# Four heads' 64x64 products at a time, three stores behind the branch, and another order of attention

## The chip, the cores and the metric

The kernel runs on one core of a Trainium2 chip. The metric is the time of one launch in microseconds (us), as the device reports it; the kernel before took 660.73 us (median of three runs, 658.44 to 661.97).

## What is computed

A linear attention with a decaying state, then two feed-forward layers; the second mixes four domains by given shares.

```python
for t in range(S):                     # B, H, S, D = 2, 8, 768, 48
    cur = einsum('bhd,bhe->bhde', u[None] * kt, vt)
    y[:, :, t] = einsum('bhd,bhde->bhe', rt, state + cur)
    state = wt[:, :, :, None] * state + einsum('bhd,bhe->bhde', kt, vt)
x = y as (1536, 384)
h = x @ w_in                           # 384 x 2048
x = where(h > 0, h, exp(min(h, 0)) - 1) @ w_out
p = domain_probs / (domain_probs.sum(-1, keepdims=True) + 1e-09)
for e in range(4):                     # w1 384 x 1024, w2 1024 x 384
    out += p[:, e:e + 1] * (maximum(x @ w1[e], 0) @ w2[e])
```

## The kernel before

**Attention** goes by 12 chunks of 128 time steps, six of each batch, taken in turn from the two batches. Eight heads lie as four pairs: a pair's two heads (48 rows each) stand on partitions 0 to 63 and 64 to 127. One chunk is a handful of pieces, each with a two-letter name in the table `ORDER`: loads of the decays (`iw`), of k and r (`ik`) and of v (`lv`); two scans on DVE (`su` L293, `pr` L301); k and r times the scans (`kd`, `rd`) and k times r (`g`); the transposed k (`tr` L316); the scores (`pa` L324), masked by `am`; the scores of a step with itself (`ow` L331: one 128x128 product for each pair, whose weights `ublock` hold u in two diagonal blocks of 64); these times v (`vo`, tile `bv`); the state's update (`pp` L358, added by `us` L365); the values (`py`: a state part L374, 64x64, then a part from the masked scores L378, 128x64, summed in one bank of PSUM); the sum with `bv` (`ys` L382); and the split of the result in two words for exact products (`xs`), spread over idle partitions by two transfers (`xd` L260).

**The first feed-forward layer** is 48 steps (four quarters of the hidden width, three blocks of four chunks, four columns each): `h` (L408, nine products of 128x512), `e` and `el` (exp, the greater of the two, the split), `z` (L429, nine products), and `dr`, which empties three banks after four steps. Its weights come in 32 pieces: `wl` loads, `wa`, `wb`, `wc` split each 64-bit word into two numbers (DVE L226, L227, ACT, POOL).

`ORDER` names every piece of the first part in the order in which each engine gets its instructions; a letter behind a number names the engine (A ACT, D DVE, P POOL, M and S mixtures for the two masks). Each engine takes its instructions strictly in that order. PSUM has eight banks: one holds limits for the scans, seven are handed out in the order in which they came free, so that a product waits for the reader of the bank that it is given. At the start `kept_busy` has PE do 11 products of 128x256 that nobody reads (L162).

**The second layer** (`experts`) is one long row of products with numbers as due times: `product` (L597, three products into a chain's bank `chain_a` to `chain_e`), `taken` (DVE or ACT reads that bank into `terms`, L609, L612, L614), `hidden_hi` (ACT) and `hidden_lo` (DVE L651), which split a hidden block into `hl`, `second` (L658, three products each), `weighted` (L667) and `added` (L673, L675). A chain's bank is written on by the next product of the chain once `taken` has read it. `load_blocks`, `split_hi` and `split_lo` prepare the weights, those of the first two blocks already beside the first layer. Nine stores (h = 7) go out from `added`, on SP's queue (L677).

At the end every engine loads a flag and branches: where decays lie out of a safe range, everything is computed again in a slower way (`recur`). With the inputs here this branch is not taken.

Of the kernel before, what the change touches and what calls it, by code (L numbers as in the profile page):

```python
# [11 lines left out]
F32 = mybir.dt.float32  # L12
# [74 lines left out]
ys9 e5 pa10 rd11P ow10 ws10A e6 dr15D pa11 el6D am10M am11S el5P py10 xs9P h7 z4 xd9 vo10 h17 g11D e7 el7P ys10 z5
xs10P ow11 vo11 h16 z6 e16 py11 e17 ys11 z7 xs11D el16P z16 xd8 xd10 dr7A h19 el17D h18 e18 xd11 | el18P e19 el19D
z17 h8 h9 e9 el9P z18 e8 el8P h11 h10 wl8 z19 e11 z8 e10 el11D wa8D el10D h21 wl11 z9 wa11D dr19D wl10 wb8P wl9 wa10D
h20 wb10D wb11P wc10D e20 z10 e21 el20D h22 wa9D z11 dr11A e22 wb9D wc8D wc11P z20 wl24 wl26 wl27 wc9D wa24D el21P  # L90
h23 el22D wa26D wb24D h24 e23 wb26D el23P z21 wa27D e24 wl25 el24P h25 z22 wa25D e25 wc26P wc24P h26 z23 el25D wl12
wl15 wb25P z24 wc25D e26 dr23D wb27D h27 wl14 wa15D el26D z25 e27 wa14D h28 wb15P e28 el27P h29 z26 wa12D wc27P el28D
h30 wb12P z27 wl28 e29 wc15D dr27D e30 wb14P wl13 wc14D el29P z28 h31 wl31 e31 el30D h32 el31D z29 e32 h35 wa13D z30
el32P wa28D wc12D wl30 wb13P e35 h33 el35D wb28P wa31D wc13P z32 e33 wl29 el33D z31 h34 wb31D dr31D wa30D wc28P wa29D
e34 h36 el34D z33 e36 el36P wb29D h37 wb30P z34 h38 wc30D e37 el37P z35 dr35D wc29P e38 z36 h39 wc31P el38P z37 h40
e40 e39 el39D el40D h41 z38 h42 e41 el41D h43 z39 e42 el42P dr39D z40 e43 h44 z41 e44 el43D h45 el44D z42 h46 e45 z43
el45P e46 el46P h47 dr43D z44 e47 z45 el47D z46 z47 dr47D
""".split()


@with_exitstack
def kernel_body(ctx, tc, wkr, vv, uu, w_in, w_out, w1, w2, dp, out):
# [145 lines left out]
    def heads_bank():  # L248
        return heads(bank())
# [674 lines left out]
```

## Time and profile before

| | us |
|---|---|
| three runs, median (lowest, highest) | 660.73 (658.44, 661.97) |
| the profiled execution, its own time | 660.07 |
| its span, first to last instruction | 658.3 |
| PE busy in the span | 638.9 |
| DVE busy | 490.6 |
| POOL busy | 362.4 |
| ACT busy | 302.2 |

The span is the time between the first and the last instruction; 1.8 us of the execution's own time lie outside it. Busy shares are means over stages with different limits: in the first 90 us DVE and PE take turns in holding the work up, later PE alone is full.

### The profile page before, as it was taken

The numbers are of one execution on the slowest core, as the hardware profiler recorded it, in microseconds if no ns is written. First come the engines' busy times: TensorE is split into PE (matmuls) and PEld (weight loads), VectorE is DVE, ScalarE is ACT, GpSimd is POOL, SyncE is SP. The second block draws the span as 40 slices with busy tenths as digits, with TensorE's granted clock in tenths as the row PEclk, the third lists the DMA queues.
The fourth block names the chain that finished last, engine by engine and source line by source line (L and its number), as shares of the span: only waits on it lengthen the run. The fifth ranks groups of instructions, "written<-read, shape, count | busy, mean of one in ns | idle before, by whom it ended". The sixth has DMA issues, their size and how long they took to land.

```text
span 658.3 us, 9122 instructions
## 1 busy us (share of the span) xinstructions
PE 638.9 (97%) x3330; PEld 524.0 (80%) x3330; DVE 490.6 (75%) x703; ACT 302.2 (46%) x582; POOL 362.4 (55%) x322
## 2 busy tenths in 40 slices
PE   7989999999999999999999999999999999999994
PEld 6878778888888778888888878878788788787883
DVE  7799999335766834599786877977967868768782
ACT  2436666455856557448343523423532434343230
POOL 5775555412242353546552765876876867744352
PEclk8789999999999999999999999999999999999998
DMA  8768550040322400001212112003130121300012
GB/s 312 220 199 289 164 174 0 17 154 1 96 73 72 144 3 1 1 0 49 88 42 72 53 53 88 25 16 105 42 104 17 41 72 34 120 0 1 0 49 102
DMA packets 20970, 50.92 MB, mean 77 GB/s; under 512 B 2680, under 2 KB 3880, under 8 KB 20916
## 3 DMA queue, kind: packets, MB, share of 16 engines
q1 hardware_dynamic: 20772, 50.25, 23.9%
q8 instruction: 28, 0.46, 0.3%
q14 instruction: 26, 0.21, 0.1%
q10 hardware_dynamic: 144, 0.00, 0.0%
HBM read 46.68 MB, written 2.38 MB: 75 GB/s over the span
## 4 chain that ended last, share of the span: by engine, by line
PE 71%; DVE 16%; issue 3%; ACT 3%; DMA 0%; SPq 0%; DVEq 0%; ACTq 0%
PE second L658 24%; PE bank L429 11%; PE bank L408 10%; PE chain_a L597 8%; PE chain_b L597 5%; PE chain_p L629 4%; PE chain_c L597 3%; PE chain_d L597 2%; DVE scaled L667 2%; PE chain_e L597 1%; DVE raw L227 1%; DVE terms L609 1%; DVE hl L651 1%; DVE e L416 1%; DVE t L226 1%
## 5 line engine op out<-in xcount | busy, mean ns | idle before, releaser
L658 PE MATMUL second<-hl,w2s 128*128 128x512 f32 x864 | 230.9, 389 | 0.1
L658 PEld LDWEIGHTS second<-hl,w2s 128*128 128x128 f32 x864 | 162.0, 188 | 34.4 <-DVE hl L190 0.5
L675 POOL TENSOR_TENSOR x<-scaled,x 128x512 f32<-128x512 f32 x60 | 86.9, 1470 | 93.2 <-DVE scaled L667 93.2
L408 PE MATMUL bank<-x,w 128*128 128x512 f32 x432 | 105.2, 392 | 1.3 <-DVE e L416 0.9
L429 PE MATMUL bank<-hl,w 128*128 128x512 f32 x432 | 105.0, 391 | 0.6 <-ACT hl L194 0.4
L651 DVE SCALAR_TENSOR_TENSOR hl<-terms,hl 128x512 fp32r<-128x512 f32 x92 | 91.5, 997 | 11.0 <-ACT hl L645 11.0
L408 PEld LDWEIGHTS bank<-x,w 128*128 128x128 f32 x432 | 80.4, 188 | 19.1 <-DVE e L416 1.5
L429 PEld LDWEIGHTS bank<-hl,w 128*128 128x128 f32 x432 | 80.6, 188 | 18.5 <-ACT hl L194 0.8
L190 POOL TENSOR_TENSOR sums<-blocks,sums 128x512 fp32r<-128x512 f32 (+1 forms) x56 | 75.3, 1356 | 26.9 <-ACT sums L194 26.9
L515 POOL TENSOR_TENSOR blocks<-blocks 128x256 f32<-128x256 f32 x84 | 71.8, 875 | 1.2 <-DMA blocks<-in_w 0.5
L190 POOL TENSOR_TENSOR hl<-e,hl 128x512 fp32r<-128x512 f32 x21 | 27.5, 1314 | 73.9 <-ACT hl L194 73.9
L612 ACT ACTIVATE terms<-chain_b 128x512 f32<-128x512 f32 x28 | 16.8, 600 | 106.1 <-PE chain_b L597 106.1
L645 ACT ACTIVATE hl<-terms 128x512 fp32r<-128x512 f32 x96 | 58.1, 623 | 14.1 <-PE second L658 6.8
L416 DVE SCALAR_TENSOR_TENSOR e<-e,bank 128x512 f32<-128x512 f32 x48 | 32.3, 681 | 39.0 <-ACT e L412 39.0
L612 ACT ACTIVATE terms<-chain_a 128x512 f32<-128x512 f32 x28 | 16.8, 598 | 80.6 <-PE chain_a L597 80.6
L597 PE MATMUL chain_a<-x,sums 128*128 128x512 f32 x168 | 47.3, 390 | 0.2 <-DVE terms L609 0.2
L411 ACT ACTIVATE e<-bank 128x512 f32<-128x512 f32 x48 | 28.4, 592 | 32.8 <-PE bank L408 29.8
L609 DVE TENSOR_TENSOR terms<-terms,chain_a 128x512 f32<-128x512 f32 x42 | 28.8, 685 | 19.1 <-PE chain_a L597 19.0
L667 DVE TENSOR_TENSOR scaled<-second,pr 128x512 f32<-128x512 f32 x60 | 40.5, 686 | 3.0 <-PE second L658 1.8
L194 ACT ACTIVATE hl<-e 128x512 fp32r<-128x512 f32 x48 | 30.0, 629 | 24.7 <-DVE e L416 21.8
L232 POOL TENSOR_TENSOR raw<-raw,t 128x384 int32<-128x384 int32 x20 | 21.7, 1099 | 33.2 <-ACT t L228 33.2
L597 PEld LDWEIGHTS chain_a<-x,sums 128*128 128x128 f32 x168 | 31.5, 188 | 7.1 <-DVE terms L609 0.6
(117 smaller groups left out, 996.8 us busy)
## 6 DMA issues: line engine op xcount, KB each, us to landing
kr<-in_wkr SPq DMA_DIRECT2D x12, 512.0 KB, 4.8
raw<-in_w_in SPq DMA_DIRECT2D x16, 384.0 KB, 3.8
raw<-in_w_out SPq DMA_DIRECT2D x16, 384.0 KB, 3.6
blocks<-in_w SPq DMA_DIRECT2D x16, 384.0 KB, 3.5
raw<-in_w SPq DMA_DIRECT2D x16, 384.0 KB, 4.2
v<-in_vv SPq DMA_DIRECT2D x12, 456.0 KB, 5.7
w<-in_wkr SPq DMA_DIRECT2D x12, 262.5 KB, 4.5
gw<-in_wkr SPq DMA_DIRECT2D x12, 262.0 KB, 2.8
```

The costliest lines, as they stand in the source:

```text
L190: engines[e].tensor_tensor(o, a, b.bitcast(F32), ALU.subtract)
L408: nc.tensor.matmul(ph, lhsT=wi[:, sa, f, kk, :], rhs=x[:, kk, c0:c0 + nch, sm], start=(kk == 0 and i == 0), stop=(kk == 2 and i == 2))
L416: nc.vector.scalar_tensor_tensor(b["e"], b["e"], -1.0, b["ph"], ALU.add, ALU.max)
L429: nc.tensor.matmul(pxs[q, bl][d][:, :cols], lhsT=wo[:, sa, f, d * P:(d + 1) * P], rhs=b["t"][:, sm], start=(f == 0 and i == 0), stop=(f == ...
L515: nc.gpsimd.tensor_tensor(*(places(blocks[u], p) for p in (r, a, c)), ALU.subtract if op == "-" else ALU.add)
L597: nc.tensor.matmul(banks[c], lhsT=weights(u, r, sa), rhs=tokens(r)[:, sm], start=r in HEADS and i == 0, stop=i == 2, skip_group_check=True)
L609: nc.vector.tensor_tensor(out, a, b, o)
L645: nc.scalar.activation(out=hls[f, b][:, 0], in_=results[f, b], func=AF.Copy if weighted else AF.Relu)
L651: nc.vector.scalar_tensor_tensor(hls[f, b][:, 1], results[f, b], 0.0, hls[f, b][:, 0].bitcast(F32), ALU.max, ALU.subtract)
L658: nc.tensor.matmul(sums[d], lhsT=w[:, sa, f, d * P:(d + 1) * P], rhs=hls[4 * h + f, b][:, sm], start=f == i == 0, stop=f == 3 and i == 2)
L667: nc.vector.tensor_tensor(o, sums[d], prs[h // 2, b], ALU.mult)
L675: nc.gpsimd.tensor_tensor(x2[:, d, s], scaled[d], x2[:, d, s], ALU.add)
```

## The change

Own scores: `ublock` is now 64 columns wide, and each head's product is 48x64 on its own quarter of the array. `QUARTERS` takes two pairs at a time, and turns the second pair round: its upper head's result goes to the lower partitions, and the other way. So four heads in a row use four different quarters of the array, two of them into one bank and two into another. The state part of the values is done in the same way; the part from the masked scores has the same products as before in another order, into the two banks. `vo` and `ys` thereby become two instructions of 128x256 each. v comes turned round from the host for the odd pairs, and rows of `w_in` are permuted to suit.

`kept_busy` is gone: a token `n2` now puts two unread products of 128x256 into the next bank that is handed out, ahead of that bank's own products. There are 14 of them in the new `ORDER`. In the second layer `hidden_lo`, where it falls due next to product 10, now comes 2.6 places later instead of 0.6; the first two blocks of its weights are split 20 places later. The last three stores stand behind the branch.

```diff
 ORDER = """
-iw0 ik0 su0 wl4 iw1 kd0D ik1 iw7 pr0 lv0 g0P su1 wa4D tr0A rd0P kd1P iw2 ow0 wb4P ik2 pa0 lv1 pr1 vo0 su2 pp0 rd1P
+wl4 wa4D iw1 iw0 su1 ik1 wl0 pr1 ik0 wb4P ik3 kd1P su0 rd1P n2 pa1 tr1A wa0D iw3 pr0 wl2 g1D lv1 rd0D iw5 n2 ow1 kd0P
...
+        for _ in range(extra.pop() if extra else 0):
+            nc.tensor.matmul(t[:, 0:IDLE], lhsT=idle[:, 0:P], rhs=idle[:, 0:IDLE], start=True, stop=True)
...
-    for p in range(NPAIR):
-        nc.scalar.activation(out=ublock[:, p], in_=half, func=AF.Copy, scale=u_sb[:, p])
+    ublock = apool.tile([P, NPAIR, 64], F32, name="ublock")
+    nc.scalar.activation(out=ublock, in_=u_sb.to_broadcast([P, NPAIR, 64]), func=AF.Copy)
...
+    QUARTERS = [[(p, j, j ^ (p & 1)) for p, j in ((2 * q, 0), (2 * q, 1), (2 * q + 1, 1), (2 * q + 1, 0))] for q in range(2)]
+
+    def half_banks():
+        return [bank()[:, 0:2 * C].rearrange("q (p c) -> q p c", p=2) for _ in range(2)]
...
         def own_scores():
-            b["po"] = heads_bank()
-            for p in range(NPAIR):
-                nc.tensor.matmul(b["po"][:, p], lhsT=ublock[:, p], rhs=b["k"][:, p], start=True, stop=True)
+            b["po"] = po = half_banks()
+            for q in range(2):
+                for p, j, o in QUARTERS[q]:
+                    nc.tensor.matmul(po[p & 1][64 * o:64 * o + 64, q], lhsT=ublock[64 * j:64 * j + D, p],
+                                     rhs=b["k"][64 * j:64 * j + D, p], start=True, stop=True)
...
         def own_values():
-            mul("D", tile_of("bv", 2), b["po"], b["v"])
-            free()
+            tile_of("bv", 2)
+            for m in range(2):
+                mul("D", b["bv"][:, m::2], b["po"][m], b["v"][:, m::2])
+                free()
...
         def values():
+            b["py"] = py = half_banks()
             if not first:
-                for p, j in both:
-                    nc.tensor.matmul(py[64 * j:64 * j + 64, p, :], lhsT=aged[64 * j:64 * j + D, D * p:D * p + 64],
-                                     rhs=b["rd"][64 * j:64 * j + D, p, :], start=p == 0, stop=False, skip_group_check=True)
+                for q in range(2):
+                    for p, j, o in QUARTERS[q]:
+                        nc.tensor.matmul(py[p & 1][64 * o:64 * o + 64, q], lhsT=aged[64 * j:64 * j + D, D * p:D * p + 64],
+                                         rhs=b["rd"][64 * j:64 * j + D, p], start=q == 0, stop=False, skip_group_check=True)
...
         def results():
-            nc.vector.tensor_tensor(b["bv"], b["py"], b["bv"], ALU.add)
-            free()
+            for m in range(2):
+                nc.vector.tensor_tensor(b["bv"][:, m::2], b["py"][m], b["bv"][:, m::2], ALU.add)
+                free()
...
-            if h == 7:
-                nc.sync.dma_start(out[d * P:(d + 1) * P, s], x2[:, d, s])
+            if h == 7 and b < 2:
+                stored(b, d)
...
-                    late = next((m + 0.6 for m in (math.ceil(k - 7.3),) if row[m][0] == "product" and row[m][2] == 10), k - 7.3)
+                    m = math.ceil(k - 7.3)
+                    late = m + 2.6 if row[m][0] == "product" and row[m][2] == 10 else k - 7.3
...
-            n = place["product", u, 0] if u > 1 else -110 + 12 * u
-            at(n - (75 if u != 2 else 112), load_blocks, u)
+            n = place["product", u, 0] if u > 1 else -90 + 12 * u
+            at(n - (75 if u > 2 else 112 if u == 2 else 95), load_blocks, u)
...
+    for d in range(3):
+        stored(2, d)
```

**PE, early attention.** Before, the values of one chunk from its masked scores (`am`), then the own scores of another (`ublock`), the update of the state and the next scores:

```order
L378 MATMUL bank_237<-am0_229,v_146 64x128
L378 MATMUL bank_237<-am1_231,v_146 64x128
L331 MATMUL bank_246<-kr_140,ublock_117 128x128 x4
L358 MATMUL bank_258<-v_188,kdt_217 64x48 x8
L324 MATMUL bank_272<-rd_251,kd_210 128x128
L324 MATMUL bank_273<-rd_251,kd_210 128x128
```

With the change, after the scores of the chunk that now comes first:

```order
L315 MATMUL bank_165<-ident_103,kd_146 128x128 x4
L136 MATMUL bank_189<-idle_87 128x256 x2
L331 MATMUL bank_189<-kr_133,ublock_113 64x128 x2
L331 MATMUL bank_192<-kr_133,ublock_113 64x128 x2
L136 MATMUL bank_203<-idle_87 128x256
L361 MATMUL bank_203<-v_183,kdt_170 64x48 x8
L381 MATMUL bank_223<-am0_217,v_183 64x128
L381 MATMUL bank_223<-am1_220,v_183 64x128
L381 MATMUL bank_224<-am1_220,v_183 64x128
L381 MATMUL bank_224<-am0_217,v_183 64x128
```

Own scores are eight products into two banks instead of four into one, and unread products (L136) stand ahead of them and of the update.

**DVE, the masks of chunk 4.** Before, the two masks of chunk 4 (`am0_556`, `am1_558`) and of chunk 5:

```order
L293 SCALAR_TENSOR_TENSOR z_506<-w_142,limits_84 128x524
L295 RECIPROCAL w_142<-z_506 128x4
L365 TENSOR_TENSOR sball_122<-sball_122,bank_478 128x192
L187 TENSOR_TENSOR am0_556<-bank_511,mask_108 128x512
L187 TENSOR_TENSOR am1_558<-bank_512,mask_108 128x512
L301 SCALAR_TENSOR_TENSOR a_560<-w_142,limits_84 128x524
L187 TENSOR_TENSOR am0_568<-bank_546,mask_108 128x512
L187 TENSOR_TENSOR am1_570<-bank_547,mask_108 128x512
```

With the change, the masks of chunk 4 (`am0_559`, `am1_561`) and the one of chunk 5 that DVE makes (`am0_614`):

```order
L179 TENSOR_TENSOR am0_559<-bank_508,mask_108 128x512
L179 TENSOR_TENSOR am1_561<-bank_511,mask_108 128x512
L368 TENSOR_TENSOR sball_115<-sball_115,bank_528 128x192
L179 TENSOR_TENSOR bv_567<-bank_539,v_361 128x2x128
L179 TENSOR_TENSOR bv_567<-bank_540,v_361 128x2x128
L292 SCALAR_TENSOR_TENSOR z_578<-w_496,limits_84 128x524
L294 RECIPROCAL w_496<-z_578 128x4
L179 TENSOR_TENSOR bv_603<-bank_593,v_448 128x2x128
L179 TENSOR_TENSOR bv_603<-bank_594,v_448 128x2x128
L179 TENSOR_TENSOR am0_614<-bank_581,mask_108 128x512
```

The own values of chunks 4 and 5, now two halves each, come ahead of chunk 5's mask; the values of chunk 5 come before those of chunk 4 on PE.

**DVE, second layer,** at the read of product 13 (L614, now L622: `terms` from `chain_a`). Before:

```order
L609 TENSOR_TENSOR terms<-chain_b,terms 128x512
L651 SCALAR_TENSOR_TENSOR hl<-terms,hl 128x512
L687 TENSOR_REDUCE ends<-gw 128x1
L614 SCALAR_TENSOR_TENSOR terms<-chain_a,terms 128x512
L651 SCALAR_TENSOR_TENSOR hl<-terms,hl 128x512
```

With the change:

```order
L617 TENSOR_TENSOR terms<-chain_b,terms 128x512
L696 TENSOR_REDUCE ends<-gw 128x1
L622 SCALAR_TENSOR_TENSOR terms<-chain_a,terms 128x512
L659 SCALAR_TENSOR_TENSOR hl<-terms,hl 128x512 x2
L617 TENSOR_TENSOR terms<-terms,chain_a 128x512
```

The split of a hidden block (`hl`) has gone from ahead of the read of `chain_a` to behind it.

## Rows read from the trace of the kernel before

**Rows 1.** The page: span; busy time of each engine, its share and its instructions.

```profile
span 658.3 us, 9122 instructions
...
PE 638.9 (97%) x3330; PEld 524.0 (80%) x3330; DVE 490.6 (75%) x703; ACT 302.2 (46%) x582; POOL 362.4 (55%) x322
```

**Rows 2.** Windows of 10 us: busy by engine, then granted clock, DMA share, GB/s.

```profile
10.00:20.00 10.00, 8.62 (x74) 7.64 (x76) 6.90 (x10) 4.62 (x13) 5.54 (x7) 0.64 0.75 270
...
40.00:50.00 10.00, 8.74 (x114) 7.32 (x114) 9.28 (x17) 4.16 (x10) 6.74 (x6) 0.83 0.29 84
...
120.00:130.00 10.00, 10.00 (x49) 8.41 (x48) 1.98 (x3) 3.50 (x6) 4.23 (x4) 1.00 0.07 20
```

**Rows 3.** The chain that ended last, 56 to 140 us: start, length, what.

```profile
57.42 0.26 DVE sball L365
...
58.61 0.28 DVE t L226
...
58.92 0.56 DVE raw L227
...
71.87 0.60 DVE bv L382
...
88.29 1.09 PE bank L331 x8
```

**Rows 4.** DVE in order of time: start, length, the masks of chunk 4.

```profile
42.26 1.28 DVE L187 TENSOR_TENSOR am<-bank,mask 128x512 f32<-128x512 f32 x2
```

**Rows 5.** PE in order of time, 113 to 119 us (two records for each product).

```profile
114.51 1.16 PE L331 MATMUL bank<-kr,ublock 128*128 128x128 f32 x8
115.60 1.16 PE L324 MATMUL bank<-rd,kd 48*128 48x128 f32 x16
116.69 1.09 PE L374 MATMUL bank<-rd,sball 48*64 48x128 f32 x16
117.71 1.09 PE L378 MATMUL bank<-am,v 128*64 128x128 f32 x16
```

**Rows 6.** The same, 39 to 46 us.

```profile
40.05 0.67 PE L358 MATMUL bank<-v,kdt 128*64 128x48 f32 x16
40.66 0.48 PE L324 MATMUL bank<-rd,kd 48*128 48x128 f32 x2
```

**Rows 7.** Who waited for whom, DVE, 8 to 53 us: total, times, longest.

```profile
DVE am L187 <- PE bank L324: 1.9, 1, 1.9
DVE bv L382 <- PE bank L378: 1.6, 2, 0.9
DVE bv L187 <- PE bank L331: 1.2, 1, 1.2
```

**Rows 8.** PE in order of time, the last of the 22 records of unread products.

```profile
6.01 2.57 PE L162 MATMUL bank<-idle 128*128 128x256 f32 x11
```

**Rows 9.** PE in order of time, second layer, 428 to 433 us.

```profile
429.98 0.86 PE L658 MATMUL second<-hl,w2s 128*128 128x512 f32 x3
431.16 0.96 PE L597 MATMUL chain_a<-xb,sums 128*128 128x512 f32 x3 [0.33 <-DVE terms L614]
431.96 0.85 PE L658 MATMUL second<-hl,w2s 128*128 128x512 f32 x3
```

**Rows 10.** The chain that ended last, 425 to 434 us.

```profile
429.13 0.79 DVE hl L651
...
430.51 0.61 DVE terms L614
...
433.50 0.68 PE second L658 x3
```

**Rows 11.** Who waited for whom, PE's weight loads, 200 to 650 us.

```profile
PEld chain_a L597 <- DVE terms L614: 4.0, 6, 0.8
```

**Rows 12.** The window from 222 to 232 us, columns as in rows 2.

```profile
222.00:232.00 10.00, 8.77 (x39) 6.61 (x37) 7.81 (x15) 6.80 (x13) 2.29 (x3) 1.00 0.73 237
```

**Rows 13.** The end: DVE's last instruction; the last store, KB, us to landing.

```profile
649.84 0.69 DVE L673 TENSOR_TENSOR x<-second,x 128x512 f32<-128x512 f32 x1 [2.03 <-PE second L658]
...
out<-x SPq DMA_DIRECT2D x1, 256.0 KB, 3.1
```

More of the change, by code (lines that the diff above doesn't have):

```diff
@@ L98 @@
+e44 h45 el44P z42 e45 h46 el45P z43 e46 el46P h47 dr43D z44 e47 z45 z46 el47D z47 dr47D
 """.split()
@@ L156, in kernel_body @@
     nc.vector.memset(idle, 1.0)
-    def kept_busy(n):
-        t = bank()
-        for _ in range(n):
-            nc.tensor.matmul(t[:, 0:IDLE], lhsT=idle[:, 0:P], rhs=idle[:, 0:IDLE], start=True, stop=True)
-        free()
-    kept_busy(WARM)
+    extra.append(WARM)
+    bank()
+    free()
     ones = const.tile([P, 49], F32, name="ones")[:, 0:1]
@@ L368, in values @@
         def values():
[L369 to L371 removed]
+            b["py"] = py = half_banks()
             if not first:
[L373 to L379 removed]
+                for q in range(2):
+                    for p, j, o in QUARTERS[q]:
+                        nc.tensor.matmul(py[p & 1][64 * o:64 * o + 64, q], lhsT=aged[64 * j:64 * j + D, D * p:D * p + 64],
+                                         rhs=b["rd"][64 * j:64 * j + D, p], start=q == 0, stop=False, skip_group_check=True)
+            for q in range(2):
+                for p, j, o in QUARTERS[q]:
+                    h = 2 * p + j
+                    nc.tensor.matmul(py[p & 1][64 * o:64 * o + 64, q], lhsT=b["vs"][:, D * h:D * h + 64], rhs=b[f"am{j}"][:, p],
+                                     start=first and q == 0, stop=True, skip_group_check=True)
         def results():
[L382 to L383 removed]
+            for m in range(2):
+                nc.vector.tensor_tensor(b["bv"][:, m::2], b["py"][m], b["bv"][:, m::2], ALU.add)
+                free()
         def parts(e):
@@ L802, in kernel_body, with turned_round, recur @@
     m0.close()
-    def recur(i, gp):
+    def turned_round(t, src):
+        for p in range(NPAIR):
+            for j in range(2):
+                o = j ^ (p & 1)
+                nc.sync.dma_start(t[64 * o:64 * o + 64, p], src[64 * j:64 * j + 64, p])
+    def recur(i, gp, u_turned):
         c = SEQ[i]
@@ L850, in kernel_body @@
             for i in range(NCH):
-                recur(i, gp)
+                recur(i, gp, u_turned)
         work.clear()
@@ L864, in kernel_body @@
         m0.close()
-ROWS = [D * h + d for k in range(3) for j in range(2) for h, ds in ((2 * k + j, range(D)), (6 + j, range(k, D, 3)))
+    for d in range(3):
+        stored(2, d)
+ROWS = [D * h + d for k in range(3) for o in range(2) for h, ds in ((2 * k + (o ^ (k & 1)), range(D)), (7 - o, range(k, D, 3)))
         for d in ds]
```

76 lines of the change are left out of this document (35 added, 41 removed).

## The prediction

> **What bounds the kernel now.** I read the page first. It shows PE busy in 638.9 of 658.3 us [rows 1], so PE has nearly no room of its own, and only two things can shorten the run: less work on PE where nothing else is late, or fewer of its waits. The profiled execution took 660.07 us against a median of 660.73; all sums below are made against 660.07.
>
> Next come the windows [rows 2]. From 10 to 20 us DVE is busy for 6.90 of 10 us and PE runs at 0.64 of its clock, which is 1.2 GHz for 7.2 us of the ten and 2.4 GHz for the rest; from 40 to 50 us DVE has 9.28 and the clock is 0.83; from 120 to 130 us DVE has 1.98 and PE is full. So attention begins with both engines waiting for each other, goes on as a stretch in which DVE is full, and ends with PE alone. The chain of waits says where one turns into the other: at 57 to 72 us its pieces are DVE's, and at 88.29 us, with an own-scores group, they have become PE's [rows 3]. A microsecond of PE saved before that point is worth nothing by itself. What counts there is how early DVE gets to a piece that PE needs, plus the PE work that is then left.
>
> In the second layer the same list has six places where PE's weight load waits for the read of `chain_a` [rows 11]. Besides, PE is idle for 1.2 us between 222 and 232 us [rows 12], and the last 7.8 us (from 649.84 + 0.69 to 658.3) hold no computing at all [rows 1, 13].
>
> **Prices on PE.** From start to start, one chunk's own scores take 115.60 - 114.51 = 1.09 us, the state part 117.71 - 116.69 = 1.02 [rows 5]. Two products of that state part already run beside each other (48x64 on two opposite quarters). No row shows four quarters in use. The bounds: half of the state part's 1.02, that is 0.51, if four run as two do now; 1.02, if they don't overlap further. I take 0.61, because 16 records of the update, with as many weight loads of the same width but fewer columns to stream, take 40.66 - 40.05 = 0.61 [rows 6]: the fastest that this trace shows 16 records to go. This saves 0.48 for own scores and 0.41 for a state part.
>
> An unread product of 128x256 is two records; eleven take 2.57 us [rows 8], so 0.47 each and 6.6 us for the 14 new ones. All stand ahead of the first layer, in PE's waits for DVE, so I cost them at nothing; the slack that hides them is counted below.
>
> **Prices on DVE.** In the chain a 512-wide read of PSUM takes 0.60 and a 192-wide one 0.26 [rows 3]; a straight line gives 0.33 for 256, so two halves take 0.66 and each split costs 0.06. There are 24 splits, 1.4 us in all.
>
> **Attention.** The clearest hand-over is the values' part that waits for a mask: chunk 4's before, chunk 5's with the change (PE now does 5 ahead of 4). Counted in the order, DVE up to and with that mask has more to do now: six own values at 0.66 instead of four at 0.60 (+1.56), four results as halves (+0.24), three products of k and r and two of r with the prefix (0.60 each, +3.0), two fewer of k with the suffix (-1.2), one more weight piece (0.28 + 0.56 = +0.84, [rows 3]) and one subtraction less for weights (about -0.5, near L227's 0.56 on the same 384 columns). Together +3.9. Ahead of it PE has the same numbers of scores, transposes, updates and values in both orders, so what is left for PE afterwards differs by the cheaper groups still to come: 6 own scores x 0.48 + 8 state parts x 0.41 = -6.2. Sum: **-2.3 us**. This is why the 10 us saved on PE over all chunks are worth a quarter of that.
>
> To this come DVE's waits. It waited 1.9 + 1.6 + 1.2 = 4.7 us for PE early on [rows 7], mostly where the clock was at its lower level [rows 2]. The unread products stand just where PE would rest. I take half of the waits away, 2.3, and give 0.5 back, because the first thing DVE needs is now a weight piece of 384 KB instead of decays of 262 KB, and the 122 KB more take 0.45 us at the 270 GB/s of these windows. So **-1.8**; the bounds are -4.7 and +3 (a later start, and POOL, which now does the masks of four of the first six chunks in part and so becomes the one waited for).
>
> On the slack: the mask ended at 42.26 + 1.28 = 43.5 us [rows 4]. It moves to 43.5 + 3.9 - 1.8 = 45.6. PE's work to that point is 8.6 us of start [rows 8] and some 29 us (6 scores at 1.09, 17 groups at 0.61, two first values at 1.03, two later ones at 1.64, 6.6 unread), 37.6 at full clock. So 8 us of cover remain: enough for the 14 unread products, or for 16 us at the lower level.
>
> **Second layer.** At one of the six places `hl` (0.79) runs ahead of the read of product 13, which ends 0.04 before `chain_a` starts [rows 9, 10]. The two triples from 429.98 to 431.96 take 1.98 us instead of 2 x 0.68: 0.62 lost. With `hl` behind it the read ends 0.79 earlier, and nothing else is late there: 6 x 0.62 = 3.7. The moved `hl` is late next. Its own product is seven places after product 10, so I give back 0.5 in all: **-3.2** (bounds -3.7 and -2).
>
> **Late first layer.** Weight splits move 20 places later, towards the four instructions on the shares, in the stretch that loses 1.2 us [rows 12]; the weight pieces around them move both ways. **0** (bounds -1.2 and +1.5).
>
> **The end.** The last store lands 3.1 us after its issue [rows 13], so some 4.6 of the 7.8 us follow the landing: the branch, and the engines' meeting. With the change SP branches earlier, beside PE's last products, but waits there for the first six stores, and issues three in a row after it. At best 2.6 of the 4.6 vanish; at worst the three stores go out late, one behind the other, +1.5. I take **-0.5**.
>
> Sum: -2.3 - 1.8 - 3.2 - 0.5 = -7.8, so **652.3 us**.
>
> **Rivals.**
>
> *Records cannot follow each other faster than now.* Both the state part (16 in 1.02) and the masked part come to 64 ns for each record [rows 5], although one uses half of the array and the other all of its rows. If that is a floor of issuing, own scores gain 0.06 and the state part nothing: 5.8 us of the 6.2 are gone, 658.1 us. Against it stand the 38 ns of a record in rows 6. The Trainium skill, in "TensorE: Matmul & The Clock Gate", section "Wait — 56ns, not 53.3ns?", states such a floor: with the hardware's decoder off, the sequencer spends about 62 ns on each matmul, which binds once the array's work is shorter. The trace speaks against it with those 38 ns; by that floor 16 records would take 0.99.
>
> *POOL or the order takes back the attention part.* POOL has more of the early products, and its instructions are twice as long. Then only the second layer and the end remain: 660.07 - 3.7 = 656.4.
>
> *Banks, the slower side.* Own scores and values now hold two of seven banks each until both halves are read, and the first layer's sums hold three for four steps. If PE, in each of the eight chunks 4 to 11, waits for the two halves of an earlier chunk (1.32) and one mask (0.60), that is 15.4 us in the stretch that is PE's alone: 667.7. It decides from 0.98 us for each chunk (7.8 / 8). For it: banks are given in the order in which they came free, and DVE is full there. Against it: at 120 us, with PE full, DVE is busy for 2 of 10 us only [rows 2].
>
> *More than forecast.* PE keeps 2.4 GHz through the start, all 4.7 us of waits go, four quarters take 0.54, the 1.2 us near 225 vanish and the end gives 2: 652.3 - 2.4 - 1.0 - 1.2 - 1.5 = 646.2.
>
> **How the numbers follow.** A change of 0.5% (3.3 us, to 657.4 or 664.0) is about what a measurement of this kernel can tell from none. The forecast has 0.62, the floor of issuing 0.10, POOL or the order 0.12, the banks 0.06, the larger gain 0.10. Of the forecast's own spread 0.04 lies above 657.4; of the 656.4 case a third does. Faster: 0.58 + 0.08 + 0.10 = 0.76; slower: the banks, 0.06; within 0.5%: the rest, 0.18. The range goes from 646.2, the larger gain, to 658.5, just over the floor of issuing.
>
> **What would show it.** Right: the own scores' 16 records in about 0.61 us and the same for the state part; the six waits of `chain_a` gone and two triples in 1.36; the early windows near full clock and DVE's waits for PE about halved; PE's first piece on the chain near 86 us. Wrong: the two groups still near 1.0; the chain in the first 60 us through POOL; PE waiting for reads by `vo` and `ys` between 60 and 130 us; a wait of `second` for `hl` in place of that of `chain_a`; or a last store that is issued more than 2 us after DVE's last instruction.

## The result, and the profile after

The changed kernel took 650.75 us (median of four runs, 649.76 to 652.48) against 660.31 for the kernel before (658.44 to 661.97): a ratio of 0.9859 with a 95% interval of 0.9824 to 0.9894, or 9.3 us less. The forecast was 652.3 us in a range of 646.2 to 658.5. The profiled execution is the slowest of the four, 652.48 us, so the profiles show 7.6 us less (660.07 to 652.48), where the sum said 7.8.

That the sum came out right is in part luck: three of the stretches below did not, and their misses (+3.1, -1.5 and -1.6 us against the forecast) cancel. Three points divide the two profiles: z20 (the start of PE's 21st group of nine products at L433, before at L429; z28 and z47 are counted in the same way, from 0), the start of the first product of `second`, and the end of PE's last product.

| stretch | before, us | after, us | difference | forecast |
|---|---|---|---|---|
| start to z20 (attention) | 171.05 | 170.06 | -0.99 | -4.1 |
| z20 to the first `second` (late first layer) | 134.97 | 133.49 | -1.48 | 0 |
| first `second` to PE's last product | 343.78 | 340.72 | -3.06 | -3.2 |
| PE's last product to the end | 8.53 | 6.46 | -2.07 | -0.5 |

The page of the changed kernel: span; busy time of each engine.

```profile
span 650.7 us, 9404 instructions
...
PE 634.5 (98%) x3454; PEld 516.1 (79%) x3454; DVE 500.2 (77%) x726; ACT 301.8 (46%) x581; POOL 358.7 (55%) x320
```

PE is busy for 4.4 us less than in [rows 1], though it has 124 more records; DVE has 9.6 us more.

Windows of the changed kernel, with the columns of [rows 2]:

```profile
10.00:20.00 10.00, 9.28 (x131) 6.99 (x131) 9.93 (x15) 4.47 (x9) 7.87 (x8) 1.00 1.01 385
20.00:30.00 10.00, 6.76 (x77) 5.45 (x74) 7.55 (x16) 4.58 (x14) 7.18 (x8) 0.74 0.78 258
...
40.00:50.00 10.00, 9.24 (x160) 7.34 (x162) 9.09 (x17) 3.69 (x12) 9.48 (x9) 1.00 0.46 144
50.00:60.00 10.00, 8.19 (x78) 6.42 (x76) 9.90 (x19) 7.21 (x16) 6.72 (x6) 1.00 0.84 272
...
222.00:232.00 10.00, 9.52 (x42) 7.40 (x41) 7.83 (x13) 6.54 (x13) 4.99 (x5) 1.00 0.59 197
```

The first stretch is what was hoped for: from 10 to 20 us DVE has gone from 6.90 to 9.93 and PE keeps 2.4 GHz (0.64 before). The next one took it back: from 20 to 30 us PE is busy for 6.76 us only, DVE for 7.55, and the clock is lower. The windows also show what goes with it: from 10 to 20 us the transfers are full (a share of 1.01, 385 GB/s against 270). In the last row PE's idle time near 225 us has fallen from 1.23 to 0.48 us [rows 12].

The chain that ended last, changed kernel:

```profile
14.85 8.31 DMA raw<-in_w_in
24.12 0.70 DVE rd L179
24.84 1.10 PE bank L361 x16
25.93 2.06 PE bank L323 x16
27.99 0.68 DVE am L179
28.72 3.82 PE bank L136 x10
...
38.88 1.59 POOL rd L179
40.48 1.59 POOL kd L179
...
83.73 0.61 DVE rd L179
84.48 1.16 PE bank L323 x16
85.64 2.27 PE bank L433 x9
```

Three things stand here that the prediction did not have. A load of a weight piece takes 8.31 us. Ten records of unread products (L136) lie on the chain for 3.82 us, most of it at the lower clock (24.8 to 31.6 us). And PE's unbroken part begins at 84.48 us, at the scores of chunk 8, not near 45 us. In the kernel before it begins at an update, just ahead of the last line of [rows 3]:

```profile
87.62 0.67 PE bank L358 x16
```

DVE's waits, 8 to 53 us (the same view as [rows 7]):

```profile
DVE bv L386 <- PE bank L381: 2.1, 1, 2.1
DVE am L179 <- PE bank L323: 1.6, 1, 1.6
DVE bv L179 <- PE bank L331: 0.8, 1, 0.8
DVE t L218 <- DMA raw<-in_w_in: 0.8, 1, 0.8
```

The same view of the kernel before has two rows more than [rows 7]:

```profile
DVE sball L365 <- PE bank L358: 0.6, 1, 0.6
DVE z L293 <- DMA w<-in_wkr: 0.2, 1, 0.2
```

So DVE waited 5.3 us for PE before (not 4.7) and 0.2 for a load, and waits 4.5 and 0.8 now: 5.5 us against 5.3, where the forecast takes away 1.8.

PE in order of time, 87 to 91 us:

```profile
87.74 0.60 PE L315 MATMUL bank<-ident,kd 128*128 128x128 f32 x4
88.27 0.67 PE L376 MATMUL bank<-rd,sball 48*64 48x128 f32 x16
88.87 1.09 PE L381 MATMUL bank<-am,v 128*64 128x128 f32 x16
89.89 0.67 PE L331 MATMUL bank<-kr,ublock 48*64 48x128 f32 x16
90.49 4.38 PE L412 MATMUL bank<-x,w 128*128 128x512 f32 x18
```

The prices were right: from start to start the state part takes 88.87 - 88.27 = 0.60 us (1.02 in [rows 5]) and the own scores 90.49 - 89.89 = 0.60 (1.09), against 0.61 chosen.

PE, 427 to 433 us (as [rows 9]), and PE's weight loads, 200 to 650 us (as [rows 11]):

```profile
427.85 0.86 PE L605 MATMUL chain_a<-xb,sums 128*128 128x512 f32 x3
428.55 0.85 PE L666 MATMUL second<-hl,w2s 128*128 128x512 f32 x3
429.23 0.84 PE L605 MATMUL chain_b<-xb,sums 128*128 128x512 f32 x3
429.91 1.52 PE L666 MATMUL second<-hl,w2s 128*128 128x512 f32 x6
431.27 0.84 PE L605 MATMUL chain_a<-xb,sums 128*128 128x512 f32 x3
```

```profile
PEld chain_b L605 <- DVE terms L617: 1.0, 5, 0.2
...
PEld chain_a L605 <- DVE terms L622: 0.5, 1, 0.5
```

The triples follow each other at 0.68 to 0.70 us, and of six waits for the read of `chain_a` one is left. The moved `hl` makes nobody late: the waits for `chain_b` were 1.1 us before and are 1.0.

The end: DVE's last instruction in order of time, and the last three stores (start of the first, us to the end of the last one's issue, queue):

```profile
644.31 0.69 DVE L682 TENSOR_TENSOR x<-second,x 128x512 f32<-128x512 f32 x1 [2.03 <-PE second L666]
```

```profile
646.01 1.47 SPq L488 DMA_DIRECT2D out<-x  x3
```

The four parts of the end are, before: 0.73 us from PE's end to DVE's, 0.02 to the start of the last store's issue, 3.15 to its landing, 4.63 from there to the end. After: 0.73, 1.97, 2.88 and 0.88. The stores go out later, since SP comes out of its branch at 645.94 only; but what followed the landing is gone.

### The profile page after: what moved, and what is told of

It is laid out like the page before. It is cut to its first block, busy times and chain, and to the rows that moved or that the text cites. A ratio compares the mean times of both kernels' runs of the same rounds, so it can differ in the third digit from the quotient of the medians.

```text
span 650.7 us, 9404 instructions
## 1 busy us (share of the span) xinstructions
PE 634.5 (98%) x3454; PEld 516.1 (79%) x3454; DVE 500.2 (77%) x726; ACT 301.8 (46%) x581; POOL 358.7 (55%) x320
## 4 chain that ended last, share of the span: by engine, by line
PE 84%; DVE 9%; DMA 3%; POOL 1%; issue 1%; SPq 0%; ACT 0%; DVEq 0%; POOLq 0%
PE second L666 28%; PE bank L433 13%; PE bank L412 12%; PE chain_a L605 9%; PE chain_b L605 6%; PE chain_p L637 4%; PE chain_c L605 3%; PE chain_d L605 3%; PE chain_e L605 1%; PE bank L323 1%; DMA raw<-in_w_in 1%; DMA kr<-in_wkr 1%; DVE hl L182 1%; DVE raw L219 1%; PE bank L381 1%
## 5 line engine op out<-in xcount | busy, mean ns | idle before, releaser
L684 POOL TENSOR_TENSOR x<-scaled,x 128x512 f32<-128x512 f32 x60 | 84.2, 1424 | 91.5 <-DVE scaled L676 91.3
L433 PE MATMUL bank<-hl,w 128*128 128x512 f32 x432 | 105.1, 391 | 0.0
L659 DVE SCALAR_TENSOR_TENSOR hl<-terms,hl 128x512 fp32r<-128x512 f32 x92 | 96.0, 1055 | 10.6 <-ACT hl L653 10.6
L433 PEld LDWEIGHTS bank<-hl,w 128*128 128x128 f32 x432 | 80.5, 188 | 17.6 <-issue 0.7
L182 POOL TENSOR_TENSOR hl<-e,hl 128x512 fp32r<-128x512 f32 x18 | 23.4, 1297 | 36.6 <-ACT hl L186 36.6
L182 POOL TENSOR_TENSOR w<-raw,w 128x384 fp32r<-128x384 f32 x21 | 22.4, 1070 | 27.6 <-ACT w L186 27.6
```

Of the source, the lines that this page charges most:

```text
L182: engines[e].tensor_tensor(o, a, b.bitcast(F32), ALU.subtract)
L433: nc.tensor.matmul(pxs[q, bl][d][:, :cols], lhsT=wo[:, sa, f, d * P:(d + 1) * P], rhs=b["t"][:, sm], start=(f == 0 and i == 0), stop=(f == ...
L659: nc.vector.scalar_tensor_tensor(hls[f, b][:, 1], results[f, b], 0.0, hls[f, b][:, 0].bitcast(F32), ALU.max, ALU.subtract)
L684: nc.gpsimd.tensor_tensor(x2[:, d, s], scaled[d], x2[:, d, s], ALU.add)
```

## The experiments

Twelve runs. Single executions of one kernel differ by 1 to 6 us, so the stretches of the profiles decide more here than the medians. Each ratio is to the kernel before, run in the same lot.

**The changed kernel once more** (`changed_again`), as a standard for the runs beside it.

> The changed kernel once more, unedited, as the standard for the runs beside it: 649.5 to 652.5 us, z20 at 168.5 to 170.1 us, 6.4 to 8.5 us from PE's last product to the end.

651.06 us (649.24 to 653.02), ratio 0.9861 (0.9823 to 0.9900). z20 at 169.13 us, then 133.52 us to the first `second` and 340.47 in the second layer, so these two stretches repeat to 0.3 us; 8.17 us of end, against 6.46. What varies is the start and the end.

### Attention

**Without the unread products.** All six `n` tokens (14 products) are taken out of the table; of the lines:

```diff
-n1 pp1 su3 g0D am1S py1 kd3D vo1 wb0P iw2 tr3A lv0 tr0A ik2 g3P pr3 rd3P pa0 lv2 am0S ys1 wl1 lv3 su2 us1 ow0 pp0 py0
+pp1 su3 g0D am1S py1 kd3D vo1 wb0P iw2 tr3A lv0 tr0A ik2 g3P pr3 rd3P pa0 lv2 am0S ys1 wl1 lv3 su2 us1 ow0 pp0 py0
```

> The changed kernel without its 14 unread products in the order of attention. Theory A, they hold the clock up in PE's waits: without them PE is at 1.2 GHz for 10 us or more in the first 50 us (6.8 us now), and DVE waits for scores longer: 652 to 655 us. Theory B, they stand in the path where the clock is low anyway: ten records of them lay on the chain for 3.82 us (28.72 to 32.47), after which DVE waited 2.06 us for the values behind them; without them that wait goes, and the time falls by 1 to 2 us: 648.7 to 649.8 us. Theory C of the prediction, they cost and bring nothing: within 0.7 us of 650.75.

651.69 us (649.46 to 654.21), ratio 0.9873 (0.9841 to 0.9905): not told apart from the changed kernel. There are signs of both A and B. Three windows of this run:

```profile
20.00:30.00 10.00, 7.00 (x104) 5.54 (x102) 9.90 (x19) 4.61 (x14) 7.39 (x9) 0.88 0.77 252
30.00:40.00 10.00, 7.86 (x114) 6.27 (x114) 9.46 (x18) 3.77 (x9) 8.78 (x9) 0.84 0.59 187
40.00:50.00 10.00, 10.00 (x108) 7.70 (x104) 7.33 (x14) 3.57 (x9) 6.71 (x7) 0.50 0.39 123
```

PE stood at 1.2 GHz for 17.1 us in the first 100 us (6.8 in the changed kernel), the whole of 40 to 50 us among them. Yet the mask of chunk 5 began at 45.55 us against 47.16, with nothing unread ahead of the values; in the six profiles with these products it begins between 44.62 and 47.16, so one profile doesn't show what that is worth. z20 came at 170.44 us against 170.06. Theory C holds in the sum, but not for the prediction's reason: the products do lie on the path, and they do hold up the clock.

**Two weight pieces loaded later.**

```diff
-wl4 wa4D iw1 iw0 su1 ik1 wl0 pr1 ik0 wb4P ik3 kd1P su0 rd1P n2 pa1 tr1A wa0D iw3 pr0 wl2 g1D lv1 rd0D iw5 n2 ow1 kd0P
-n1 pp1 su3 g0D am1S py1 kd3D vo1 wb0P iw2 tr3A lv0 tr0A ik2 g3P pr3 rd3P pa0 lv2 am0S ys1 wl1 lv3 su2 us1 ow0 pp0 py0
-pr2 xs1P ws3A wc0P ik4 us0 iw4 vo0 xd1 ow3 wa1D rd2D wa2D lv4 pp3 pa3 am3D wb1P wb2P vo3 n5 py3 su4 ys0 ws2A ys3 wl16
+wl4 wa4D iw1 iw0 su1 ik1 wl0 pr1 ik0 wb4P ik3 kd1P su0 rd1P n2 pa1 tr1A wa0D iw3 pr0 g1D lv1 rd0D iw5 n2 ow1 kd0P
+n1 pp1 su3 g0D am1S py1 kd3D vo1 wb0P iw2 tr3A lv0 tr0A ik2 g3P pr3 rd3P pa0 lv2 am0S ys1 lv3 wl2 wl1 su2 us1 ow0 pp0 py0
+pr2 xs1P ws3A wc0P ik4 us0 iw4 vo0 xd1 ow3 rd2D lv4 pp3 pa3 am3D vo3 wa1D wa2D wb1P wb2P n5 py3 su4 ys0 ws2A ys3 wl16
```

> The changed kernel with two loads of weight pieces (the pieces wl2 and wl1) moved on SP's queue to behind the load of v of chunk 3, and their splits on DVE (wa1, wa2) to behind chunk 3's own values. Theory A, the transfers are late: in the profile of the changed kernel PE stands still from 22.7 to 24.8 us, and v of chunk 3 landed at 24.70; the lower clock follows from 24.8 to 31.6 us. With 768 KB out of its way (at 385 GB/s 2.0 us) v lands near 22.7, the wait of 2.1 us goes, and if the clock then stays at 2.4 GHz DVE's mask of chunk 5 (ended at 47.8) ends 2 to 4 us earlier: 647 to 649 us against 650.75. Theory B, DVE's own work binds there and the wait is only moved: the splits cost the same later, the mask ends within 0.7 us of 47.8, 650 to 651.5 us.

653.28 us (650.46 to 653.69), ratio 0.9885 (0.9858 to 0.9913): nothing gained. PE in order of time, 22 to 33 us:

```profile
23.44 0.67 PE L361 MATMUL bank<-v,kdt 128*64 128x48 f32 x16
...
25.98 2.43 PE L136 MATMUL bank<-idle 128*128 128x256 f32 x10 [0.78 <-DVE am L179]
...
31.96 1.37 PE L323 MATMUL bank<-rd,kd 48*128 48x128 f32 x16 [1.93 <-POOL kd L179]
```

The mechanism of A is right: v landed at 23.18 us (24.70 in the changed kernel) and the 2.1 us in front of the update (L361) are gone. But 8 us later PE waits 1.93 us for POOL, whose work on the two pieces, ahead of `kd` in both orders, now comes later (`kd` starts at 30.73 us instead of 28.05), and the clock was at 1.2 GHz for 10.2 us all the same (12.3 to 15.7, 32.8 to 39.6). z20 came at 169.08 us, within what the changed kernel itself shows. B is the better account: the wait moved on.

**Own scores twice, ahead of the hand-over and behind it.** In chunks 0 to 5 (shown), or with `i >= 6` in chunks 6 to 11, each product is issued twice.

```diff
-            for q in range(2):
+            for q in [0, 1] * (2 if i < 6 else 1):
                 for p, j, o in QUARTERS[q]:
                     nc.tensor.matmul(po[p & 1][64 * o:64 * o + 64, q], lhsT=ublock[64 * j:64 * j + D, p],
```

> The changed kernel with every product of the own scores of chunks 0 to 5 (those ahead of the hand-over from DVE to PE) issued twice, the second over the first: 6 x 0.60 = 3.6 us more work for PE. The prediction's claim: PE's time before the hand-over is worth nothing, so at most 0.7 us more, 650.7 to 651.5 us. Rival: PE and DVE wait for each other in turns there, so that PE's time counts where DVE waits for it (8.0 us of waits in all): 1.5 to 3.6 us more, 652.2 to 654.4 us.

> The same for chunks 6 to 11, behind the hand-over: again 3.6 us more work for PE. The prediction's claim: there PE alone counts, so all of it is lost, 654.0 to 654.6 us. Rival: DVE still binds up to 90 us, where the own scores of chunks 6 and 7 lie, so a third of it is hidden: 2.4 us, 653.1 us.

Early: 650.49 us (648.68 to 652.20), ratio 0.9845 (0.9817 to 0.9873). Late: 652.87 us (650.47 to 654.91), ratio 0.9879 (0.9852 to 0.9905). The price of the doubling was wrong in both expectations. PE in order of time in the second run:

```profile
89.37 1.10 PE L331 MATMUL bank<-kr,ublock 48*64 48x128 f32 x32
90.41 1.88 PE L412 MATMUL bank<-x,w 128*128 128x512 f32 x7
```

32 records take 1.04 us where 16 take 0.60, so the second sixteen cost 0.44 and six chunks 2.6 us in place of 3.6. Of these 2.6 us the early run shows 0.2 (z20 at 170.16 us; three profiles of the same attention with as long a time at the lower clock have it at 169.82 to 170.06, mean 169.95) and the late one 1.45 (171.40). (As long, but not at the same places.) So PE's time before the hand-over is worth next to nothing here. And behind it only part counts: four of the six late groups stand behind 84.5 us (89.89, 95.40, 114.76 and 123.55 in the changed kernel), 4 x 0.44 = 1.8 us; the own scores of chunks 6 and 7, at 62.7 and 73.2 us, cost nothing. The profile bears this out: chunk 8's scores began at 84.02 us in the late run, no later than the 84.48 of the changed kernel, and from there to z20 it took 87.38 us in place of 85.58, 1.8 more. PE had no room left, though: the chain is PE's alone from 59.10 us on in that run.

**DVE's product of own scores and v twice, chunks 0 to 5.**

```diff
             for m in range(2):
-                mul("D", b["bv"][:, m::2], b["po"][m], b["v"][:, m::2])
+                for _ in range(2 if i < 6 else 1):
+                    mul("D", b["bv"][:, m::2], b["po"][m], b["v"][:, m::2])
                 free()
```

> The changed kernel with the product of own scores and v made twice on DVE in chunks 0 to 5 (two instructions of 128x256 more for each, 0.67 us, 4.0 us in all). Own scores issued twice by PE in the same chunks cost 0 us (650.49). Theory A, DVE alone binds from the start to about 84 us: its waits (8 us, most of them before its first mask) take up little, and 3 to 4 us are lost: 653.7 to 654.8 us, the last product of attention's masks 3 to 4 us later. Theory B, DVE's waits for PE and for transfers take up half of it: 1.5 to 2.5 us, 652.2 to 653.2. Theory C, neither engine binds, the transfers do: under 1 us, below 651.7.

653.72 us (652.50 to 656.49), ratio 0.9919 (0.9890 to 0.9948): 2.7 us more than the changed kernel's 651.06, which ran in another lot (by the two ratios it is 3.8); near A. Its profiled execution was the fastest of its six and shows less: z20 at 170.89 us, 0.94 behind that mean of 169.95, and DVE idle for 6.4 of the first 84 us, against 8.9 to 9.8 in those three profiles, so part of the added work fell into its waits. So a microsecond of DVE ahead of the hand-over costs 0.2 to 0.7 us (0.94 and 2.7 of 4.0), one of PE 0.1 (0.2 of 2.6). That DVE alone binds there isn't shown; that it binds more than PE is.

**The clock, from all profiles with the changed kernel's attention.** Time at 1.2 GHz in the first 100 us, and z20:

| kernel | at 1.2 GHz, us | z20, us |
|---|---|---|
| stores on ACT's queue | 0.0 | 167.53 |
| stores inside | 3.4 | 168.50 |
| changed, again | 3.4 | 169.13 |
| blocks early | 6.8 | 169.82 |
| split near | 6.8 | 169.97 |
| changed | 6.8 | 170.06 |
| before, stores behind (old attention) | 10.2 | 170.79 |
| before (old attention) | 13.7 | 171.05 |

In the first six rows nothing of attention differs. Their spread of 2.5 us goes with the clock, though at 3.4 us two of them still differ by 0.6. Why the clock falls in one execution and not in the next these profiles don't show. In the changed kernel's profile the clock fell at 24.8 us, while PE stood still for 2.1 us; in the first row's, PE stood still for 2.4 us (25.1 to 27.5) and it did not fall. There the ten unread records took 2.43 us, in the changed kernel's profile 3.82. The spread lies wholly ahead of the hand-over: chunk 8's scores begin at 81.94 to 84.48 us in these six, and from there to z20 each takes 85.58 to 85.60 us.

### Late first layer and second layer

**The first two blocks at their old due times.**

```diff
-            n = place["product", u, 0] if u > 1 else -90 + 12 * u
-            at(n - (75 if u > 2 else 112 if u == 2 else 95), load_blocks, u)
+            n = place["product", u, 0] if u > 1 else -110 + 12 * u
+            at(n - (75 if u != 2 else 112), load_blocks, u)
```

> The changed kernel with the first two blocks of the second layer's weights at their old due times, 20 places earlier. In the changed kernel the stretch from the values' product number 28 to the last of the first layer (z28 to z47) takes 74.33 us, before 75.81. Theory A, the moved weights are why: 75.5 to 75.9 us with them back, 652.2 us in all. Theory B, the new order of the first layer's own weights: 74.0 to 74.6, 650.75 within 0.5.

654.72 us (651.94 to 655.82), ratio 0.9918 (0.9885 to 0.9951). From z28 to z47 it took 76.81 us, more than the 75.81 of the kernel before. PE's weight loads in this run, 200 to 300 us:

```profile
PEld bank L412 <- DVE e L420: 2.1, 2, 1.3
PEld bank L433 <- DVE hl L182: 1.5, 1, 1.5
```

These 3.6 us were 1.2 in the changed kernel (0.9 for `e`, 0.3 for a `hl` of POOL). A holds, beyond its own number: 76.81 - 74.33 = 2.5 us lie in the moved weights, and the rest of the new order costs 1.0 us here without them. DVE's waits show what the old due times do. Before, and in this run (180 to 240 us):

```profile
DVE sums L190 <- ACT sums L194: 6.2, 3, 2.4
```

```profile
DVE sums L182 <- ACT sums L186: 5.1, 3, 2.4
```

DVE stands still until ACT has made its half of a split (`sums`); PE then waits at 207.53 us for an `e` and at 215.22 for a `hl` of DVE. In the changed kernel DVE has no such wait there. That these waits alone make up the 2.5 us is not shown.

**The split of a hidden block at its old due time.**

```diff
-                    late = m + 2.6 if row[m][0] == "product" and row[m][2] == 10 else k - 7.3
+                    late = m + 0.6 if row[m][0] == "product" and row[m][2] == 10 else k - 7.3
```

> The changed kernel with the split of a hidden block at its old due time (0.6 in place of 2.6 behind product 10). The prediction's claim: six reads of product 13's bank are late again by 0.62 us each, so from the first product of the second layer to PE's last one it takes 340.72 + 3.1 = 343.8 us, as in the kernel before, and 653.9 us in all. Rival: part of the gain came from another part of the change (the moved weights, another order of DVE): 341.5 to 343 us for this layer.

653.75 us (652.20 to 657.19), ratio 0.9901 (0.9868 to 0.9935). From the first `second` to PE's last product: 343.81 us, where 343.8 was expected. The six waits are back:

```profile
PEld chain_a L605 <- DVE terms L622: 4.3, 6, 0.8
```

### The end

**All stores inside**, as before the change.

```diff
-            if h == 7 and b < 2:
+            if h == 7:
                 stored(b, d)
...
-    for d in range(3):
-        stored(2, d)
```

> The changed kernel with all nine stores issued ahead of the branch, as before. In the profile of the changed kernel 6.46 us lie between PE's last product (644.27) and the end of the span (650.73), in the kernel before 8.53 (649.80 to 658.33). Theory A, the branch hides the fetch beside PE's last products: with the stores back inside the last 2.1 us are lost again, 8.4 to 8.6 us of end and 652.3 to 653.3 us in all. Theory B of the prediction, the stores' place is worth 0.5 us: 6.9 to 7.1 us of end, 651.0 to 651.5. Theory C, the end varies with the landing of the last store whatever the place (8.46 in the run with later loads, 8.2 with late own scores twice): the end is 7 to 8.5 and the median within 1 us of 650.75.

652.28 us (651.88 to 652.92), ratio 0.9887 (0.9863 to 0.9912); 7.80 us of end, of which 3.95 follow the last landing. No theory fits whole: the end is that of C, the median that of A.

**The kernel before, with its last three stores behind the branch.**

```diff
-            if h == 7:
+            if h == 7 and b < 2:
                 nc.sync.dma_start(out[d * P:(d + 1) * P, s], x2[:, d, s])
...
+    for d in range(3):
+        nc.sync.dma_start(out[d * P:(d + 1) * P, 1024:1536], x2[:, d, 1024:1536])
```

> The kernel before with its last three stores behind the branch, and nothing else of the change. From PE's last product to the end of the span it took 8.53 us before; with stores behind the branch 6.46 to 8.46 us in the seven runs so far (mean 7.5), with all stores inside the changed kernel 7.80. Theory A, the move is worth 2.1 us: 6.3 to 6.6 us of end. Theory C, what it gives is mostly the spread of the last store's landing: 6.5 to 8.5 us, a median 0 to 1.5 us below the kernel before's. It also shows the old order of attention a second time: the product z20 at 171.05 us in the first profile; 170 to 172 if the early part varies as in the changed kernel (168.5 to 170.1 in four profiles).

658.61 us (656.18 to 661.93) against 660.77 beside it, ratio 0.9982 (0.9954 to 1.0010): not resolved. 7.31 us of end. C is right for the most part: ten profiles with the stores behind the branch on SP's queue have ends of 6.46 to 8.46 us, mean 7.43; two with the stores inside 8.53 and 7.80. That is a gain of 0.7 us, well inside the spread of 2 us, where the changed kernel's profile happened to show 2.07. The spread is mostly the last store's: it landed 2.88 us after its issue in the changed kernel, 3.95 in the second profile of it, 4.27 in the run with later loads; its issue came 2.7 to 3.5 us after PE's last product.

**The last three stores on ACT's queue.**

```diff
-        nc.sync.dma_start(out[d * P:(d + 1) * P, s], x2[:, d, s])
+        (nc.scalar if b == 2 else nc.sync).dma_start(out[d * P:(d + 1) * P, s], x2[:, d, s])
```

> The changed kernel with its last three stores on ACT's queue in place of SP's. On SP the first of them is issued at 646.01, 1.0 us after DVE's last sum, since SP's branch (643.36) had to fetch what follows it (645.94), and the last at 646.97. ACT is through its branch before 640 us. Theory A, the fetch of SP holds the stores back: on ACT each store goes out when its sum is ready, the last at about 645.1, and lands 1.9 us earlier; 4.8 to 6.5 us of end, 1.5 to 2 us less in all than the changed kernel beside it. Theory B, PE's and DVE's own branches (PE's took 3.53 us, to 647.99) set the end: no more than 0.5 us less. Theory C, ACT's branch waits for the landings of its queue in the same way: nothing gained.

650.47 us (649.57 to 651.28) against 651.06: not told apart. The stores in order of time in this run:

```profile
642.47 2.31 ACTq L488 DMA_DIRECT2D out<-x  x3
```

The first went out 0.09 us after DVE's last sum (642.38), 0.9 us sooner than on SP, but not before it: behind the branch all three wait for DVE's last instruction, though two of the sums were ready earlier (636.93 and 639.66 us). The three issues then took 2.31 us in place of 1.47, so the last came 1.81 us behind DVE's sum, against 1.97 on SP, and landed 3.03 us later; the end took 6.46 us. A's cause is there, but its gain is not. B's number is nearer, but not its cause: PE's branch was over at 645.19 us, and the span still ended 0.89 us behind the last landing (647.22). Medians 0.6 us apart don't settle more.

**Stores on ACT's queue and the later loads together.**

> Stores on ACT's queue, and the two loads of weight pieces behind the load of v of chunk 3 (as in the run with later loads, where PE's last product came at 642.78 against 644.27, but the last store landed 4.27 us after its issue). Theory A, both gains are real and add up: 2 to 3.5 us less than the changed kernel beside it, 647 to 649 us. Theory B, the early gain is the clock's chance (it was 1.2 GHz for 10.2 us there, 6.8 us in the changed kernel) and z20 falls anywhere between 168.5 and 170.1: no less than with the stores on ACT alone.

650.62 us (649.42 to 651.36), ratio 0.9858 (0.9820 to 0.9896); z20 at 169.22 us with 10.2 us at the lower clock, 6.18 us of end. B. No version here beats the changed kernel by more than can be measured.

## Why the prediction was right, and where its steps failed

**Prices on PE: right.** 0.60 for both groups against 0.61. The floor of issuing at 64 ns for each record falls: 16 records in 0.60 us are 38 ns each, and those that a doubling adds 27 ns. The Trainium skill ("TensorE: Matmul & The Clock Gate", section "Wait — 56ns, not 53.3ns?") gives about 62 ns for each matmul with the hardware's decoder off; the 27 to 38 ns of these traces are below that, and no run here shows how the decoder was set.

**"Chunk 5's mask is the hand-over": the step that failed.** The mask was the clearest place where PE waits for DVE, but not the last. Behind it DVE stays full and PE does not (8.19 of 10 us from 50 to 60), and the chain goes over to PE at 84.48 us. Before the change it had gone over at 87.62, next to the own-scores group of [rows 3], and the prediction had read it there; the sum then counted cheaper groups from 45 us on all the same. Behind 84.48 us there are four own scores and four state parts, 4 x 0.48 + 4 x 0.41 = 3.6 us, not six and eight with 6.2. The runs with doubled own scores show it: two late groups out of six cost nothing. The hand-over came 3.1 us sooner, with 3.6 us less work for DVE ahead of it (74.7 us busy against 78.3). PE from there to z20 took 85.58 us in place of 83.43: the new order leaves one more group of scores, of masked values and of transposes behind the hand-over (+2.65), the first layer's products take 0.6 more, and four cheap own scores and state parts take 1.1 less than three dear ones of each did. Together that is the -0.99.

Counted at the mask, as the prediction did, its two terms look better than they are. The mask ended 4.3 us later (43.55 to 47.84), where +2.1 was forecast, and from there to z20 it took 5.3 us less, where -6.2 was. PE was indeed busy for 6.1 us less behind the mask (125.8 to 119.6), but what it saves between mask and hand-over is not on the path.

**"The unread products stand just where PE would rest": failed.** `n5` fills the bank that is handed out next, and that bank comes free with the mask of chunk 3. So the ten records stand behind PE's wait for the mask, not in it, and ahead of the values that DVE needs next: 2.43 us on the path at full clock, 3.82 mostly at the lower one. They do hold the clock up (6.8 us low against 17.1), and by the one profile without them that is worth about as much as they cost. The slack of 8 us that was counted for them is a slack of PE's whole work to that point; it does not lie at that place.

**"-1.8 of DVE's waits": nothing of it in the profiled pair.** DVE had 5.3 us of waits from 8 to 53 us, against 5.5. Up to the mask its work grew by 3.2 us (35.3 to 38.4 busy; +3.9 was counted) and its idle time by 1.1 (8.3 to 9.4), where the forecast has -1.8. The bound of "a later start" was thought of for the first load alone (2.68 us, 0.6 more than before). The load that mattered was v of chunk 3, issued at 17.08 us behind four weight pieces (`wl4`, `wl0`, `wl2`, `wl1`) and landed at 24.70, just when PE went on. The list of waits names DVE's `rd` for this (L361, 2.1 us), which that instruction does not need; in the run with the stores inside the same wait reads as what it is:

```profile
24.24 0.67 PE L361 MATMUL bank<-v,kdt 128*64 128x48 f32 x16 [1.52 <-DMA v<-in_vv]
```

Over all profiles attention gained more: z20 at 169.17 us in the mean of six against 170.92 in two, -1.75 us, still under half of the 4.1.

**Late first layer, 0: wrong, -1.48.** The moved splits did come near the four instructions on the shares: in the changed kernel they lie at 205.6 to 209.4 and 218.1 to 220.2 us, the shares at 213.2 to 216.2. They gained 2.5 us all the same, where the rest of the order lost 1.0; the waits that went are DVE's for `sums`, 6.2 us in the kernel before. The prediction named the place, the 1.2 us [rows 12] and both bounds, and then set gain against loss without a row for either.

**Second layer, -3.2: right** (-3.06), by the mechanism named: with the old due time the six waits and 3.09 us are back.

**The end, -0.5: near in the mean (-0.7, two profiles against ten, so not resolved), short by 1.6 in the pair.** What follows the last landing fell from 4.63 us to 0.88, as thought; the stores, issued later, lose 1.95 us of that again.

**The rivals.** POOL did become one of those waited for (38.48 to 42.07 and 43.26 to 45.69 us on the chain), and attention gave back 3.1 of the 4.1 us that were forecast. So this rival came near: with nothing from the late first layer and 0.5 from the end the profile would have stood at 660.07 - 0.99 - 3.06 - 0.5 = 655.5 us. Banks: from 60 to 130 us PE waited 0.7 us in all for DVE, 0.5 of it for `rd` and 0.2 for a `bv`, so no sign of it. The profiled executions of the changed kernel were the slowest of their lots twice (652.48 of 649.76 to 652.48; 653.02 of 649.24 to 653.02). The profiles therefore account for 7.6 of the 9.3 us; the table of the clock shows how an execution can be 2.5 us shorter, but the faster ones have no profile, and that is where the rest stays open.

## What to carry to other kernels

Find the last place where the chain goes from one engine to the other, and count work saved on the second engine from there, not from the first clear wait; doubling a group on either side measures this in two runs. Count too what a new order moves across that place. Work that only keeps an engine awake belongs into a bank that is free before the wait, or it stands behind the wait and in the way. When an early stage is re-ordered, follow the loads too: a full transfer queue makes late what is asked for last, and the list of waits can name another engine for it.

## What was not expected of the hardware

Products on four different quarters of the array start together: in the trace their records come in fours, 6 to 7 ns apart, and the fours 89 ns behind that, 109 ns in all. A sequence of them costs 27 ns a record once it runs, and 0.16 us for each change between groups. (The Trainium skill, "TensorE: Matmul & The Clock Gate", section "Measured speedup vs the span model", counts about 4 ns of issuing for each further product on another part of the array; this trace has 6 to 7.)

Stores of 256 KB of the same form, the last work of the same program, landed 2.50 to 4.27 us after their issue over the fourteen profiles (2.79 to 4.27 on SP's queue, 2.50 and 3.03 on ACT's): these last microseconds vary by more than the move of the stores was worth.
